# Retention and a mixture of experts on one core: q's factors computed on the chip, one tile's keys transposed instead of loaded, and a new order of work where the two stages meet

## The chip, the cores and the metric

The kernel runs on one core of one Trainium2 chip. The metric is the device time of one execution in microseconds (us), given as the median over several runs; the profile shows one execution.

The engines are TensorE (PE: matmuls; PEld are its loads of stationary operands, which overlap them), VectorE (DVE), ScalarE (ACT), GpSimd (POOL) and SyncE (SP, which here only issues transfers). Each works through its own instructions in order and waits on semaphores for the others.

## The reference

```python
def _attn_ref(q, k, v):                      # 8 batches, 8 heads, 576 positions, 64 per head
    scores = (1 / np.sqrt(D_)) * np.matmul(q, k.transpose(0, 1, 3, 2))
    gamma = 1.0 - 2.0 ** (-5.0 - np.arange(H))
    rel = pos[:, None] - pos[None, :]
    Dmat = np.where(rel >= 0, gamma[:, None, None] ** rel, 0.0)
    return np.matmul(scores * Dmat, v)       # retention: decay by distance, causal

def _moe_ref(x, w_gate, w_output_gate, w1, w2):   # x: 4608 tokens of 512; 8 experts, 1024 hidden
    logits = x @ w_gate
    e_idx = np.argmax(logits, axis=1)             # one expert per token
    gate_w = softmax(logits)[np.arange(N), e_idx]
    eom = sigmoid(x @ w_output_gate)
    for e in range(E):
        mask = e_idx == e
        ye = np.maximum(x[mask] @ w1[e], 0.0) @ w2[e]
        out[mask] = gate_w[mask, None] * eom[mask, e, None] * ye
```

## The kernel before

**Stage 1, retention.** The 4608 tokens are 36 tiles of 128 (`g` from 0 to 35); nine of them cover two sequences of 576 positions, so `c = g % 9` tells where a tile lies in its pair (`c = 4` holds the end of one and the start of the other, `c = 8` needs no update of the state). For each tile `load` brings `pk[g]`: q, k and v, q and k transposed. `scores` multiplies k by q into the PSUM tile `sc` (two banks), and VectorE masks it into `S_sb`. `by_state` adds what earlier tiles left in a running state, `outT` adds the tile's own part into `o_ps`, and VectorE multiplies `o_ps` by the decay factors of q, `gq_sb`, into `xT`. Those factors depend on the position in the sequence, so before the change five sets of 128 columns are loaded (one for each of `c` = 0 to 4; later tiles use columns shifted by 64). `update` adds the tile to the state with `kn[g]`, the keys by rows, and ScalarE copies the state out of PSUM (`stT`). `kn` comes in one of two ways: for odd `g` between 2 and 31 (`by_rows`) it is loaded by `load_k`, otherwise `k_rows` transposes it on TensorE into the one bank `k_ps` and ScalarE copies it. `prep` scales v on GpSimd (`vp`). `xnat` turns `xT` back into rows and forms the gating logits; ScalarE copies the rows into `xgrp`.

**Gating.** Every four tiles, `gate1a`, `gate1b`, `gate2`, `gate3a` and `gate3b` choose an expert and a slot for each token with small VectorE operations; `gate2` counts with matmuls into `k_ps`. The rows go by indirect scatters on GpSimd into `xs` in DRAM, which is ordered by expert. `gate4` works out which slots stay empty and adds scatters that fill them.

**Stage 2, experts.** An expert's rows are read back, transposed, and split into a high part `xh` (ScalarE) and a lower part `xl` (VectorE), and so are the weights; `mm1` makes three products for each block of weights (`xh`·`w1h`, `xl`·`w1h`, `xh`·`w1l`) and `mm2` likewise with `w2`. Each hidden block passes through ScalarE (`hh`) and VectorE (`hl`). The results are scattered to `out`.

**Where the stages meet.** Expert 0 starts before the last tiles are gated: its first 360 rows are three row tiles, transposed during the last three tiles of stage 1 by `transp(0, 0)`, `transp(0, 1)` and `transp(0, 2)`. `transp_hi` does the four transposes into a PSUM tile named by `pools["x_ps"]` and the high part, `transp_lo` the lower part. The first goes into `k_ps`, the second into the second bank of `sc`, the third into the first bank of `sc`. After them come `by_state(35)`, `outT(35)`, `xnat(34)` and the first `mm1(0, 0, 0)`, whose PSUM tiles lie where `sc`, `o_ps` and `k_ps` were.

**What sets the order.** In stage 1 and at the meeting (`tc.manual_schedule`), each engine executes instructions in the order in which the program writes them; only GpSimd's order is chosen by the scheduler at the meeting. All of SP's transfers go through one queue. Transfers take eight semaphores in turn, so that a transfer's issue waits until the eighth before it has landed. The start is written out in `load_first`; the rest of the constants follow in `load_rest(step)` at tiles 0 to 3.

Of the kernel before, what the change touches and what calls it, by code (L numbers as in the profile page):

```python
# [10 lines left out]
F32 = mybir.dt.float32  # L11
# [3 lines left out]
AF = mybir.ActivationFunctionType  # L15
ALU = mybir.AluOpType
# [17 lines left out]
TA = -(-CA // P)  # L34
SNAP = 5
# [13 lines left out]
def tile_retention_moe(  # L49
# [16 lines left out]
    V, A, G, T, SP = nc.vector, nc.scalar, nc.gpsimd, nc.tensor, nc.sync  # L66
# [16 lines left out]
    gk_sb = con_sb[:, 0:CPB * H].rearrange("p (c h a) -> p c h a", c=CPB, a=1)  # L83
    cmat_sb = con_sb[:, CPB * H:].rearrange("p (c a i) -> p c a i", c=4, a=1)
    ident = cmat_sb[:, 2, 0, :]
    gq_sb = const.tile([P, NP, 640], F32, name="gq_sb")
    iw = const.tile([P, NP, 144], F32, name="iw")
    cbf_sb = const.tile([P, 2, P], BF16, name="cbf_sb")
    csm_sb = const.tile([P, 16 + 2 * CT], F32, name="csm_sb")
    base2 = const.tile([P, 1, E], F32, name="base2")  # L90
    bump = const.tile([P, 1], F32, name="bump")
    tok_sb = const.tile([P, NTILE], I32, name="tok_sb")
# [8 lines left out]
    base = csm_sb[:, 8:16].rearrange("p (a e) -> p a e", a=1)  # L101

    stT = [const.tile([P, NP, D], F32, name=f"stT{i}") for i in range(2)]

    def load_rest(step):
        if step < 3:
            n = slice(P * (step + 2), P * (step + 3))
            SP.dma_start(out=gq_sb[:, :, n], in_=gq[:, :, n])
        if step == 0:
            for p in range(NP):  # L110
                o = 0 if p % 2 == 0 else 16
                A.copy(out=iw[:, p, o:o + P], in_=ident)
# [12 lines left out]
    const.tile([P, 16], F32, name="shift0")  # L125
    W1, W2 = {}, {}

    def start_w(which, e, fp):
# [92 lines left out]
    def transp(e, t):  # L221
        transp_lo(*transp_hi(e, t))
# [88 lines left out]
    def load_first():  # L311
        t = [ld.tile([P, 3, 512], F32, name="pk") for _ in range(4)]
        pk.update(enumerate(t))
        n = CPB * H + 2 * P
        SP.dma_start(out=t[0][:, 1], in_=pack[0, :, 1])
        A.dma_start(out=t[0][:, 0], in_=pack[0, :, 0])
        SP.dma_start(out=con_sb[:, 0:n], in_=cmat[:, 0:n])
        A.dma_start(out=t[0][:, 2], in_=pack[0, :, 2])
        SP.dma_start(out=con_sb[:, n:n + P], in_=cmat[:, n:n + P])
        A.dma_start(out=t[1][:, 0:2], in_=pack[1, :, 0:2])  # L320
        SP.dma_start(out=gq_sb[:, :, 0:P], in_=gq[:, :, 0:P])
        SP.dma_start(out=t[1][:, 2], in_=pack[1, :, 2])
        for i in (2, 3):
            if i == 3:
                SP.dma_start(out=gq_sb[:, :, P:2 * P], in_=gq[:, :, P:2 * P])
            SP.dma_start(out=t[i][:, 0:2], in_=pack[i, :, 0:2])
            SP.dma_start(out=t[i][:, 2], in_=pack[i, :, 2])
            if i == 2:
                wgv = wg.rearrange("(p c) g -> c p g", c=P)
                SP.dma_start(out=iw[:, 0:NP:2, P:144], in_=wgv[:, 0:NP:2])  # L330
                SP.dma_start(out=iw[:, 1:NP:2, 0:16], in_=wgv[:, 1:NP:2])

    def by_rows(g):
        return g % 2 == 1 and 1 < g < GT * SNAP + 12
# [77 lines left out]
    def outT(g, S_sb, state):  # L412
        o = o_ps
        c = g % CPB
        part = lambda p, r: o[64 * ((p + r) % 2):64 * ((p + r) % 2) + 64, r, P * (p // 2):P * (p // 2) + P]

        for r, p in ((r, p) for r in range(2) for p in range(NP)):
            T.matmul(part(p, r), lhsT=vs[g][:, 2 * p + r, :], rhs=S_sb[:, r, p, :],
                     start=(state is None and p < 2), stop=True, skip_group_check=True)
        x = wk.tile([P, NP, P], F32, name="xT")  # L420
        c0 = P * c if c < 5 else 64 + P * (c - 5)
        V.tensor_tensor(out=x.rearrange("p (r s) i -> p r s i", r=2),
                        in0=o[:, :, 0:2 * P].rearrange("p r (s i) -> p r s i", s=2),
                        in1=gq_sb[:, :, c0:c0 + P].rearrange("p (r s) i -> p r s i", r=2), op=ALU.mult)
        xT[g] = x

    def gate1a(n):
# [62 lines left out]
    def gate3b():  # L490
        n, oh, ex, zs = gt.pop("pend")
        sli = gt.pop("sl")
        x = xgrp[n % 2]
# [6 lines left out]
        V.reciprocal(out=x[:, :, DM + 1:DM + 2], in_=zs)  # L500
# [68 lines left out]
    pools["x_ps"] = lambda: ps_s.tile([P, NP, P], F32, name="k_ps").rearrange("p (b k) i -> p b k i", b=2)  # L569
    def scatters(n, pause):  # L570
        for f in todo[0:n]:

# [4 lines left out]
    with tc.manual_schedule():  # L577
        S_next = scores(0)
        k_rows(0)
        for g in range(NTILE):  # L580
# [15 lines left out]
            if g + 1 < NTILE:  # L596
                prep(g + 1)
                S_next = scores(g + 1)
            else:
                pools["x_ps"] = lambda: sc[:, 0].rearrange("p (b k i) -> p b k i", b=2, k=2)  # L600
                transp(0, 2)
            if g < NTILE - 1:

# [20 lines left out]
            weights_lo(g - 1, (1,))  # L624
            if g > 0:
                xnat(g - 1)
            if "sl" in gt:
                gate3b()
            if "fill" in gt and g == NTILE - 2:
                gate4()  # L630
            if g % GT == 0 and g > 0:
                gate1a(g // GT - 1)
            if g == NTILE - 1:
                wide = wk.tile([P, H, D], F32, name="vp")
            if g == NTILE - 1:
                scatters(len(todo), wide)
            if g in (NTILE - 3, NTILE - 2):
                if g == NTILE - 2:
                    pools["x_ps"] = lambda: sc[:, 1].rearrange("p (b k i) -> p b k i", b=2, k=2)
                transp(0, g - NTILE + 3)  # L640
    gt["after"] = list(scat)
    psctx.close()
    ps_h = mctx.enter_context(tc.tile_pool(name="ps_h", bufs=4, space=PSUM, side="right", reuse_waits="tile"))
# [196 lines left out]

def _consts():
    gam = 1.0 - 2.0 ** (-5.0 - np.arange(H, dtype=np.float64))
    s = np.concatenate([np.arange(S), np.arange(64)])
    gqh = gam[:, None] ** s[None, :] / np.sqrt(D)
    gq = np.repeat(gqh[np.array(SLOT)][:, :, None], D, axis=2).reshape(NP, P, 640).transpose(1, 0, 2)
    pos = (np.arange(CPB)[None, :] * P + np.arange(P)[:, None]) % S
# [52 lines left out]
```

## Time and profile before

| | |
|---|---|
| median of 3 runs | 612.72 us (611.83 to 613.25) |
| profiled execution, its own time | 608.3 us |
| span of that execution | 606.5 us |
| mean granted TensorE clock | 0.991 |
| busy: PE, PEld | 591.2 us (97%), 529.4 us (87%) |
| busy: DVE, ACT, POOL | 332.0 us (55%), 221.3 us (36%), 188.0 us (31%) |
| moved by transfers | 100.28 MB, mean 165 GB/s |
| stage 1 / stage 2 meet at | about 153 to 162 us from the span's start |

In the rows of the profile a line stands as L235; a line of the timeline gives start, duration, engine, line, operation, output <- inputs, how many instructions were merged, and in brackets the idle time before it and what ended it ("issue" is time in which nothing that the profile shows was waited for). The view of waits gives total, number and longest. The table by windows gives, for each stretch, the busy time of each engine, then the granted clock, the share of the 16 transfer engines that was busy (it can pass 1, since packets overlap) and GB/s. "PEld" rows are used for TensorE below where possible, since starts of loads are measured and ends of matmuls are modelled.

### The profile page before, as it was taken

Reading aid. Unit: us, or ns where it says so; the run is one execution under the profiler, and the core shown is the slowest. Engines: PE = TensorE matmul, PEld = TensorE weight load, DVE = VectorE, ACT = ScalarE, POOL = GpSimd, SP = SyncE. Lnnn points to the kernel's source line nnn. Section 1 sums busy time; section 2 is a strip of 40 time slices with the busy share of each in tenths; the row PEclk is TensorE's granted clock in tenths of the full one; section 3 lists DMA queues with packets and bytes.
Section 4 is the critical chain, followed back from the end, with each engine's and each line's share of the span. In section 5 each row is a group of like instructions: output and inputs, shape, how many; then the busy total and the mean of one; then the engine's idle time right before and its main releaser. Section 6 shows DMA issues by size and latency. Waiting matters only on the chain. (4 is left out here: it accounts for less than half of the span.)

```text
span 606.5 us, 13987 instructions
## 1 busy us (share of the span) xinstructions
PE 591.2 (97%) x5688; PEld 529.4 (87%) x5688; DVE 332.0 (55%) x731; ACT 221.3 (36%) x481; POOL 188.0 (31%) x235
## 2 busy tenths in 40 slices
PE   8899999999899999999999999999999999999995
PEld 6789889889798999879978987997899799889974
DVE  3498989898460666625543554445265435625410
ACT  3233444333231544325333443443354344325110
POOL 2245555575636524016013301601250110110011
PEclk9999999999799999999999999999999999999998
DMA  9988999995215676434343634444262335321011
GB/s 312 356 306 329 322 308 328 346 308 165 90 57 192 177 198 194 140 118 135 110 138 116 175 104 136 116 139 139 96 189 91 121 102 146 100 83 52 1 38 42
DMA packets 56925, 100.28 MB, mean 165 GB/s; under 512 B 14839, under 2 KB 35832, under 8 KB 56860
## 3 DMA queue, kind: packets, MB, share of 16 engines
q1 hardware_dynamic: 46988, 76.72, 39.9%
q0 software_dynamic: 9440, 21.60, 9.8%
q8 instruction: 45, 0.74, 0.5%
q10 hardware_dynamic: 432, 1.05, 0.5%
q14 instruction: 20, 0.16, 0.1%
HBM read 77.75 MB, written 31.18 MB: 180 GB/s over the span
## 5 line engine op out<-in xcount | busy, mean ns | idle before, releaser
L262 PE MATMUL h_ps<-xh,w1h 128*128 128x360 f32 (+1 forms) x512 | 155.4, 303 | 0.0
L262 PE MATMUL h_ps<-xh,w1l 128*128 128x360 f32 (+1 forms) x512 | 155.0, 303 | 0.0
L262 PE MATMUL h_ps<-xl,w1h 128*128 128x360 f32 (+1 forms) x512 | 154.9, 303 | 0.0
L289 POOL DMA_INDIRECT out_dram<-y,idx x40 | 39.7, 993 | 314.5 <-ACT y L288 269.5
L270 DVE SCALAR_TENSOR_TENSOR hl<-h_ps,hh 128x360 fp32r<-128x360 f32 (+1 forms) x128 | 61.3, 479 | 129.0 <-ACT hh L269 123.2
L283 PE MATMUL y_ps<-w2h,hh 128*128 128x512 f32 (+1 forms) x320 | 125.1, 391 | 0.0
L283 PE MATMUL y_ps<-w2l,hh 128*128 128x512 f32 (+1 forms) x320 | 125.0, 391 | 0.0
L283 PE MATMUL y_ps<-w2h,hl 128*128 128x512 f32 (+1 forms) x320 | 124.7, 390 | 0.0
L269 ACT ACTIVATE hh<-h_ps 128x360 fp32r<-128x360 f32 (+1 forms) x128 | 54.7, 427 | 118.0 <-PE h_ps L262 117.1
L262 PEld LDWEIGHTS h_ps<-xl,w1h 128*128 128x128 f32 x512 | 96.3, 188 | 0.3
L262 PEld LDWEIGHTS h_ps<-xh,w1h 128*128 128x128 f32 x512 | 96.3, 188 | 0.3
L262 PEld LDWEIGHTS h_ps<-xh,w1l 128*128 128x128 f32 x512 | 96.2, 188 | 0.0
L288 ACT ACTIVATE y<-y_ps,idx 128x512 f32<-128x512 f32 (+1 forms) x40 | 27.5, 688 | 138.8 <-issue 90.1
L147 DVE TENSOR_TENSOR w1l<-st,w1h 128x512 fp32r<-128x512 f32 x64 | 47.3, 776 | 48.2 <-ACT w1h L142 46.8
L283 PEld LDWEIGHTS y_ps<-w2h,hl 128*128 128x128 f32 (+1 forms) x320 | 58.8, 184 | 14.1
L283 PEld LDWEIGHTS y_ps<-w2h,hh 128*128 128x128 f32 (+1 forms) x320 | 58.9, 184 | 13.8
L283 PEld LDWEIGHTS y_ps<-w2l,hh 128*128 128x128 f32 (+1 forms) x320 | 58.8, 184 | 13.6
L354 POOL TENSOR_TENSOR vp<-pk,con_sb 128x512 f32<-128x512 f32 x36 | 37.4, 1040 | 54.5 <-PE st_ps L394 34.9
L194 POOL DMA_INDIRECT xs<-xgrp,sli x36 | 39.0, 1082 | 33.0 <-issue 17.1
L194 POOL DMA_INDIRECT xs<-zx,fill x42 | 45.2, 1077 | 7.1 <-issue 6.6
L147 DVE TENSOR_TENSOR w2l<-st,w2h 128x512 fp32r<-128x512 f32 x64 | 44.7, 736 | 2.3
L378 DVE TENSOR_TENSOR S_sb<-sc,con_sb 128x512 f32<-128x512 f32 x64 | 41.1, 683 | 7.1 <-PE sc L367 6.6
(128 smaller groups left out, 672.4 us busy)
## 6 DMA issues: line engine op xcount, KB each, us to landing
st<-in_w_dram SPq DMA_DIRECT2D x64, 512.0 KB
pk<-in_pack_dram SPq DMA_DIRECT2D x32, 768.0 KB
x_q<-xs SPq DMA_DIRECT2D x140, 64.0 KB
kn<-in_krow_dram SPq DMA_DIRECT2D x14, 256.0 KB
gq_sb<-in_gq_dram SPq DMA_DIRECT2D x5, 256.0 KB
pk<-in_pack_dram SPq DMA_DIRECT2D x4, 256.0 KB
pk<-in_pack_dram SPq DMA_DIRECT2D x2, 512.0 KB
x_g<-xs SPq DMA_DIRECT2D x4, 256.0 KB
```

The costliest lines, as they stand in the source:

```text
L147: V.tensor_tensor(out=lo[:, k], in0=st[:, k], in1=hi[:, k].bitcast(F32), op=ALU.subtract)
L194: i = G.indirect_dma_start(out=xs, out_offset=bass.IndirectOffsetOnAxis(ap=at, axis=0), in_=x, in_offset=None, **({} if bound is None else ...
L262: i = T.matmul(ps, lhsT=a[:, k, :], rhs=b[:, k, 0:n], start=(j == 0), stop=(j == 3 * KB - 1))
L269: A.activation(out=hh, in_=ps, func=AF.Relu)
L270: V.scalar_tensor_tensor(out=hl, in0=ps, scalar=0.0, in1=hh.bitcast(F32), op0=ALU.max, op1=ALU.subtract)
L283: i = T.matmul(ps, lhsT=a[:, n], rhs=b, start=(j == 0), stop=(j == 3 * FB - 1))
L288: A.activation(out=y, in_=ps, func=AF.Copy, scale=idx.bitcast(F32)[0:m, e, t, 1:2])
L289: G.indirect_dma_start(out=out, out_offset=bass.IndirectOffsetOnAxis(ap=idx[0:m, e, t, 0:1], axis=0), in_=y, in_offset=None, bounds_check= ...
L354: G.tensor_tensor(out=vs[g], in0=pk[g][:, 2].rearrange("p (h d) -> p h d", h=H), in1=gk_sb[:, g % CPB].broadcast_to([P, H, D]), op=ALU.mult)
L378: V.tensor_tensor(out=v(S_sb[:, r].rearrange("p a i -> p (a i)")), in0=v(sc[:, r]), in1=cmat_sb[:, 0:2].rearrange("p c a i -> p a (c i)"). ...
```

## The change

**q's factors.** `gq` is now one set of 128 by 512 plus a 16-column table `gam`. ScalarE makes sets 1 to 4 from set 0 at steps 0 to 3 of `load_rest`, each with four activations of 128 columns that multiply by one column of `gam` (step 3: eight of 64 columns, half of them by `back`, four columns that come with `csm_sb`). The positions of k's factors are shifted so that five sets serve all tiles (`c % 5`). Four loads of 256 KB go; the first becomes 128 rows of 2 KB, and `gam` (8 KB) is loaded ahead of tile 2.

**Tile 3's keys.** `by_rows` starts at 5, so tile 3's `kn` is transposed on TensorE and copied by ScalarE, and its load of 256 KB goes.

**The meeting.** The third row tile goes into `k_ps`. `gate3b` loses its tail (`gate3c`: the running counts `cum`), which for group 7 comes in tile 35's iteration together with `gate4`, so that VectorE does the lower parts first.

```diff
     def load_rest(step):
-        if step < 3:
-            n = slice(P * (step + 2), P * (step + 3))
-            SP.dma_start(out=gq_sb[:, :, n], in_=gq[:, :, n])
+        for k in range(NP):
+            n = P if step < 3 else 64
+            A.activation(out=gq_sb[:, step + 1, P * k:P * k + n], in_=gq_sb[:, 0, P * k:P * k + n], func=AF.Copy,
+                         scale=gam[:, NP * step + k:NP * step + k + 1])
+            if step == 3:
+                A.activation(out=gq_sb[:, 4, P * k + 64:P * k + P], in_=gq_sb[:, 0, P * k + 64:P * k + P],
+                             func=AF.Copy, scale=back[:, k:k + 1])
...
-        SP.dma_start(out=gq_sb[:, :, 0:P], in_=gq[:, :, 0:P])
+        SP.dma_start(out=gq_sb[:, 0], in_=gq[:, 0:DM])
         SP.dma_start(out=t[1][:, 2], in_=pack[1, :, 2])
         for i in (2, 3):
-            if i == 3:
-                SP.dma_start(out=gq_sb[:, :, P:2 * P], in_=gq[:, :, P:2 * P])
+            if i == 2:
+                SP.dma_start(out=gam, in_=gq[:, DM:DM + 16])
...
     def by_rows(g):
-        return g % 2 == 1 and 1 < g < GT * SNAP + 12
+        return g % 2 == 1 and 3 < g < GT * SNAP + 12
...
-                        in1=gq_sb[:, :, c0:c0 + P].rearrange("p (r s) i -> p r s i", r=2), op=ALU.mult)
+                        in1=gq_sb[:, c % 5].rearrange("p (r s i) -> p r s i", r=2, s=2), op=ALU.mult)
...
         todo.extend(partial(scatter_x, x[:, t, :], sli[:, t, :]) for t in range(GT))
+        gt["cum"] = (n, oh)
+        if n != NTILE // GT - 2:
+            gate3c()
+
+    def gate3c():
+        n, oh = gt.pop("cum")
...
             else:
-                pools["x_ps"] = lambda: sc[:, 0].rearrange("p (b k i) -> p b k i", b=2, k=2)
+                pools["x_ps"] = k_bank
                 transp(0, 2)
...
-            if "sl" in gt:
+            if "sl" in gt and g != NTILE - 2:
                 gate3b()
-            if "fill" in gt and g == NTILE - 2:
-                gate4()
...
             if g == NTILE - 1:
                 wide = wk.tile([P, H, D], F32, name="vp")
-            if g == NTILE - 1:
+                gate3c()
+                gate4()
                 scatters(len(todo), wide)
             if g in (NTILE - 3, NTILE - 2):
                 if g == NTILE - 2:
                     pools["x_ps"] = lambda: sc[:, 1].rearrange("p (b k i) -> p b k i", b=2, k=2)
-                transp(0, g - NTILE + 3)
+                x = transp_hi(0, g - NTILE + 3)
+                if "sl" in gt:
+                    gate3b()
+                transp_lo(*x)
```

TensorE (PE) where the stages meet, before: `x_g` are expert 0's rows, L235 the transposes of row tiles 1 and 2, L262 the first products of `mm1`.

```order
L531 MATMUL xb<-iw,xT 128x144 x2
L235 MATMUL sc<-con_sb,x_g 128x128 x4
L235 MATMUL sc<-con_sb,x_g 128x104 x4
L409 MATMUL o_ps<-pk,stT_93 64x128 x8
L418 MATMUL o_ps<-S_sb,vp 64x128 x8
L531 MATMUL xa<-iw,xT 128x144 x2
```

And after, at the same place (line numbers move: L235 is now L241, L409 is L415, L418 is L424, L531 is L542):

```order
L542 MATMUL xb<-iw,xT 128x144 x2
L241 MATMUL sc<-con_sb,x_g 128x128 x4
L241 MATMUL k_ps<-con_sb,x_g 128x104 x4
L415 MATMUL o_ps<-pk,stT_93 64x128 x8
L424 MATMUL o_ps<-S_sb,vp 64x128 x8
L542 MATMUL xa<-iw,xT 128x144 x2
```

The order on TensorE is the same; only the bank into which the last four transposes write has changed.

VectorE (DVE) at the same place, before: from `gate3b`'s last operation for the scattered rows, the reciprocal, through `gate3c`'s and `gate4`'s work (`ohs` to `fill`), to the lower parts `xl` of row tiles 1 and 2.

```order
L500 RECIPROCAL xgrp_91<-zs 128x4
L506 TENSOR_REDUCE ohs<-oh 128x8
L507 TENSOR_TENSOR cum<-cum,ohs 128x8
L515 TENSOR_TENSOR cnt<-cnt,bump 128x1
L207 TENSOR_TENSOR fl<-cnt,csm_sb 128x3
L212 TENSOR_TENSOR fo<-fl,csm_sb 128x3
L213 TENSOR_SCALAR fo<-fo 128x3
L217 TENSOR_TENSOR fl<-fl,fo 128x3
L218 TENSOR_TENSOR fill_2860<-fl,csm_sb 128x3
L245 TENSOR_TENSOR xl_2757<-sc,xh_2756 128x4x128
L245 TENSOR_TENSOR xl_2757<-sc,xh_2756 128x4x104
L422 TENSOR_TENSOR xT<-o_ps,gq_sb 128x512
```

And after, from the same reciprocal on:

```order
L505 RECIPROCAL xgrp_91<-zs 128x4
L251 TENSOR_TENSOR xl_2779<-sc,xh_2778 128x4x128
L251 TENSOR_TENSOR xl_2779<-k_ps,xh_2778 128x4x104
L427 TENSOR_TENSOR xT<-o_ps,gq_sb 128x512
L551 COPY lg<-xa 128x16
L552 TENSOR_TENSOR lg<-xb,lg 128x16
L517 TENSOR_REDUCE ohs<-oh 128x8
L518 TENSOR_TENSOR cum<-cum,ohs 128x8
L526 TENSOR_TENSOR cnt<-cnt,bump 128x1
```

Eight operations have moved from ahead of the two lower parts to behind `xT` and the logits of tile 34.

ScalarE (ACT) at the start, before: `k_ps` to `kn` is the copy of transposed keys, `iw` the identity that `xnat` uses, `stT` the state.

```order
L350 COPY kn<-k_ps 128x512
L112 COPY iw<-con_sb 128x128 x4
L396 COPY stT_93<-st_ps 128x256
L350 COPY kn<-k_ps 128x512
L396 COPY stT_94<-st_ps 128x256
```

And after:

```order
L356 COPY kn<-k_ps 128x512
L111 ACTIVATE gq_sb<-gq_sb,gam 128x128 x4
L119 COPY iw<-con_sb 128x128 x4
L402 COPY stT_93<-st_ps 128x256
L356 COPY kn<-k_ps 128x512
L111 ACTIVATE gq_sb<-gq_sb,gam 128x128 x4
L402 COPY stT_94<-st_ps 128x256
```

The activations stand ahead of the copies of the state in ScalarE's order; the first four need the loads of set 0 and of `gam`.

More of the change, by code (lines that the diff above doesn't have):

```diff
@@ L85, in tile_retention_moe @@
     ident = cmat_sb[:, 2, 0, :]
-    gq_sb = const.tile([P, NP, 640], F32, name="gq_sb")
+    gq_sb = const.tile([P, 5, DM], F32, name="gq_sb")
     iw = const.tile([P, NP, 144], F32, name="iw")
     cbf_sb = const.tile([P, 2, P], BF16, name="cbf_sb")
-    csm_sb = const.tile([P, 16 + 2 * CT], F32, name="csm_sb")
+    csm_sb = const.tile([P, 20 + 2 * CT], F32, name="csm_sb")
     base2 = const.tile([P, 1, E], F32, name="base2")
@@ L103, in tile_retention_moe @@
     stT = [const.tile([P, NP, D], F32, name=f"stT{i}") for i in range(2)]
+    gam = const.tile([P, 16], F32, name="gam")
+    back = csm_sb[:, 16 + 2 * CT:]
     def load_rest(step):
-        if step < 3:
-            n = slice(P * (step + 2), P * (step + 3))
-            SP.dma_start(out=gq_sb[:, :, n], in_=gq[:, :, n])
+        for k in range(NP):
[5 more added lines that the diff above has]
+                             func=AF.Copy, scale=back[:, k:k + 1])
         if step == 0:
@@ L121, in load_rest @@
             G.memset(zx.bitcast(I32)[:, DM:DM + 1], NT)
-    const.tile([P, 16], F32, name="shift0")
     W1, W2 = {}, {}
@@ L420, in outT @@
         x = wk.tile([P, NP, P], F32, name="xT")
-        c0 = P * c if c < 5 else 64 + P * (c - 5)
         V.tensor_tensor(out=x.rearrange("p (r s) i -> p r s i", r=2),
                         in0=o[:, :, 0:2 * P].rearrange("p r (s i) -> p r s i", s=2),
-                        in1=gq_sb[:, :, c0:c0 + P].rearrange("p (r s) i -> p r s i", r=2), op=ALU.mult)
+                        in1=gq_sb[:, c % 5].rearrange("p (r s i) -> p r s i", r=2, s=2), op=ALU.mult)
         xT[g] = x
@@ L567, in tile_retention_moe, with k_bank @@
     every = {mybir.EngineType.PE, mybir.EngineType.Activation, mybir.EngineType.DVE, mybir.EngineType.SP}
-    pools["x_ps"] = lambda: ps_s.tile([P, NP, P], F32, name="k_ps").rearrange("p (b k) i -> p b k i", b=2)
+    def k_bank():
+        return ps_s.tile([P, NP, P], F32, name="k_ps").rearrange("p (b k) i -> p b k i", b=2)
+    pools["x_ps"] = k_bank
     def scatters(n, pause):
@@ L599, in tile_retention_moe @@
             else:
-                pools["x_ps"] = lambda: sc[:, 0].rearrange("p (b k i) -> p b k i", b=2, k=2)
+                pools["x_ps"] = k_bank
                 transp(0, 2)
@@ L842, in _consts @@
     gam = 1.0 - 2.0 ** (-5.0 - np.arange(H, dtype=np.float64))
[L843 to L846, printed above, removed]
+    slots = lambda a: np.repeat(a[np.array(SLOT)][:, :, None], D, axis=2).reshape(NP, P, -1).transpose(1, 2, 0)
+    gq = slots(gam[:, None] ** np.arange(P)[None, :] / np.sqrt(D)).transpose(0, 2, 1).reshape(P, DM)
+    gt = slots(gam[:, None] ** (P * np.arange(1, 5))[None, :]).reshape(P, 4 * NP)
+    back = slots(gam[:, None] ** float(-P)).reshape(P, NP)
+    pos = np.arange(CPB)[None, :] * P + np.arange(P)[:, None]
+    pos = np.where(pos < S, pos, pos - S - 64)
     gk = gam[None, None, :] ** (-pos[:, :, None].astype(np.float64))
@@ L852, in _consts @@
     cbf = np.stack([(j < i), np.ones((P, P))], axis=1)
-    csm = np.zeros((P, 16 + 2 * CT))
+    csm = np.zeros((P, 20 + 2 * CT))
+    csm[:, 16 + 2 * CT:] = back
     csm[:, 16:16 + CT] = P * np.arange(CT)[None, :] + np.arange(P)[:, None]
-    csm[:, 16 + CT:] = [NT] + [CAP] * (CT - 1)
+    csm[:, 16 + CT:16 + 2 * CT] = [NT] + [CAP] * (CT - 1)
     csm[:, 0:8] = np.arange(8, 0, -1)
@@ L860, in _consts @@
     return {
-        "gq": np.ascontiguousarray(gq.astype(f)),
+        "gq": np.concatenate([gq, gt], axis=1).astype(f),
         "cmat": np.concatenate([gk.reshape(P, CPB * H), cmat.reshape(P, 4 * P)], axis=1).astype(f),
```

## The prediction

> **What bounds the kernel now.** I read the waits of TensorE first, because it is busy 97% of the span (table above): only time in which it stands still or runs slowly can be won. Its largest wait that is not at the start, by the starts of weight loads (total, number, longest), and the others that the change can touch:
>
> ```profile
> PEld o_ps L418 <- issue: 5.7, 27, 1.2
> PEld sc L235 <- DVE xl L245: 3.2, 1, 3.2
> PEld st_ps L394 <- DMA kn<-in_krow_dram: 1.2, 1, 1.2
> ```
>
> There is one wait of 3.2 us, for VectorE, where the transposes of expert 0's third row tile are due, and one of 1.2 us for the keys of a tile. Next the table by windows around the first one (busy us and count of PE, PEld, DVE, ACT, POOL, then the granted clock):
>
> ```profile
> 154.00:156.00 2.00, 0.00 (x0) 0.00 (x0) 1.79 (x12) 0.00 (x0) 0.95 (x1) 0.91 0.00 0
> ...
> 160.00:162.00 2.00, 2.00 (x11) 1.84 (x8) 0.76 (x2) 0.37 (x1) 1.77 (x3) 0.50 0.51 201
> 162.00:164.00 2.00, 2.00 (x12) 2.00 (x12) 0.28 (x2) 0.37 (x1) 1.84 (x3) 0.89 0.47 184
> ```
>
> The gap costs twice: the granted clock begins to fall inside it (0.91), and TensorE then works at 0.50 until shortly after 162 us. So I read the timeline of the weight loads there, a clean tile first and then the gap:
>
> ```profile
> 149.24 0.47 PEld L409 LDWEIGHTS o_ps<-pk,stT 64*64 64x64 f32 x16
> 149.88 0.85 PEld L418 LDWEIGHTS o_ps<-S_sb,vp 128*64 128x64 f32 x16 [0.17 <-issue]
> 150.70 0.60 PEld L394 LDWEIGHTS st_ps<-vp,kn 128*64 128x64 f32 x16
> ...
> 151.61 0.54 PEld L531 LDWEIGHTS xa<-iw,xT 128*128 128x128 f32 x4
> 152.09 0.56 PEld L531 LDWEIGHTS xb<-iw,xT 128*128 128x128 f32 x4
> 152.58 0.56 PEld L235 LDWEIGHTS sc<-con_sb,x_g 128*128 128x128 f32 x4
> 156.30 0.65 PEld L235 LDWEIGHTS sc<-con_sb,x_g 104*128 104x128 f32 x4 [3.15 <-DVE xl L245]
> 157.20 0.73 PEld L409 LDWEIGHTS o_ps<-pk,stT 64*64 64x64 f32 x16 [0.25 <-issue]
> 158.26 1.57 PEld L418 LDWEIGHTS o_ps<-S_sb,vp 128*64 128x64 f32 x16 [0.33 <-POOL vp L573]
> 160.16 0.98 PEld L531 LDWEIGHTS xa<-iw,xT 128*128 128x128 f32 x4 [0.33 <-issue]
> 161.05 1.06 PEld L531 LDWEIGHTS xb<-iw,xT 128*128 128x128 f32 x4
> 162.01 0.34 PEld L262 LDWEIGHTS h_ps<-xh,w1h 128*128 128x128 f32 x1
> ```
>
> The same instructions take about twice as long after the gap (L418 1.57 against 0.85 us). The gap itself ends with VectorE's first lower part, which stands behind the tail of gating:
>
> ```profile
> 152.48 0.15 DVE L480 COPY cnt<-k_ps 128x1 f32<-128x1 f32 x1
> ...
> 154.10 0.18 DVE L500 RECIPROCAL xgrp<-zs 128x4 f32<-128x4 f32 x1
> 154.19 0.18 DVE L506 TENSOR_REDUCE ohs<-oh 128x8 f32<-128x32 bf16 x1
> ...
> 155.48 0.16 DVE L218 TENSOR_TENSOR fill<-fl,csm_sb 128x3 int32<-128x3 f32 x1
> 155.56 0.68 DVE L245 TENSOR_TENSOR xl<-sc,xh 128x512 fp32r<-128x512 f32 x1
> 157.84 0.59 DVE L245 TENSOR_TENSOR xl<-sc,xh 128x416 fp32r<-128x416 f32 x1 [1.60 <-ACT xh L241]
> ```
>
> Both banks of `sc` are one tile, so the transposes into the first bank waited until VectorE had read the second.
>
> **The meeting of the stages (term A).** Before, TensorE needs from 152.58 to 162.01 = 9.43 us from the second row tile's transposes to the first product of expert 0. After, the third row tile goes to `k_ps`, whose last reader before it is the copy of the count, done at 152.48 + 0.15 = 152.63; the transposes are due at 152.58 + 0.56 = 153.14, so 0.5 us of margin. At full clock the same work is: two sets of transposes at 0.6 (0.56 and a little) = 1.2; L409 to L418 0.64 (149.24 to 149.88); L418 to the next group 0.82 (149.88 to 150.70); `xa` 0.48 (151.61 to 152.09); `xb` 0.49 (to 152.58): 3.63, say 3.65 us. That is a gain of 5.8 us, of which 3.15 is the gap and the rest the slow clock; the first products lose a little more in the half clock, so I take A = -5.9. Its cover: the first products at about 156.2 need both lower parts. VectorE, after the reciprocal at 154.28, needs 0.68 + 0.59 and is done at 155.55, 0.7 us early. The eight moved operations are 155.64 - 154.19 = 1.45 us; behind tile 34's logits they end near 158.6, ahead of the first `hl` at about 159 and of the fill scatter, GpSimd's fifth of the chain, that needs them. Ends for A: -3.15, if only the gap goes and the clock falls all the same; -6.2, if the smaller transposes (104 columns) are cheaper than I put them.
>
> [...]
>
> **Tile 3 (terms B and C).** Weight loads at tile 3, and the largest pause without a cause in the view of waits between 60 and 150 us:
>
> ```profile
> 21.68 0.20 PEld L418 LDWEIGHTS o_ps<-S_sb,vp 128*64 128x64 f32 x4 [1.21 <-issue]
> 23.05 0.55 PEld L394 LDWEIGHTS st_ps<-vp,kn 128*64 128x64 f32 x16 [1.17 <-DMA kn<-in_krow_dram]
> 23.66 0.42 PEld L348 LDWEIGHTS k_ps<-con_sb,pk 128*128 128x128 f32 x4
> ...
> PEld sc L367 <- issue: 0.7, 1, 0.7
> ```
>
> B: the load of tile 3's keys goes, and with it 1.17 us of waiting; four transposes come, 0.42 us on TensorE. ScalarE's extra copy falls into a stretch where it waits for TensorE. B = -0.75. C: the pause of 1.21 us at 21.68 has no cause in the profile. It stands where the transfer engines are fullest, and five transfers of 256 KB, 1.3 MB, go from ahead of it; but pauses of up to 0.7 us come later too, under a smaller load. Ends: 0 (it stays) and -1.2. By the nearest row, 0.7, I let it shrink to about half: C = -0.6.
>
> **ScalarE makes the factors (term D).** The rows at the start, and two durations for the price of a column as the factor:
>
> ```profile
> 7.28 0.90 ACT L112 COPY iw<-con_sb 128x128 f32<-128x128 f32 x4
> 8.68 1.04 POOL L354 TENSOR_TENSOR vp<-pk,con_sb 128x512 f32<-128x512 f32 x1 [2.00 <-DMA pk<-in_pack_dram]
> 9.75 0.37 ACT L396 COPY stT<-st_ps 128x256 f32<-128x256 f32 x1 [1.58 <-PE st_ps L394]
> 11.14 0.47 PEld L409 LDWEIGHTS o_ps<-pk,stT 64*64 64x64 f32 x16
> 13.39 0.37 ACT L396 COPY stT<-st_ps 128x256 f32<-128x256 f32 x1 [2.47 <-PE st_ps L394]
> ...
> L350 ACT COPY kn<-k_ps 128x512 f32<-128x512 f32 x18 | 10.5, 585 | 9.1 <-PE k_ps L348 6.2 <-DMA kn<-in_krow_dram 2.5
> L288 ACT ACTIVATE y<-y_ps,idx 128x512 f32<-128x512 f32 x2 | 1.4, 688 | 9.8 <-PE y_ps L283 9.8
> ```
>
> A factor per row costs 688 - 585 = 0.10 us more. The four copies of 128 columns take 0.90, so four such activations take about 1.3. [...] From 8.5: factors to 9.8, `iw` to 10.7, `stT` 0.37 to 11.07, needed at 11.14. There is no margin left, so each 0.1 us by which `gam` is later costs 0.1: behind it in ScalarE's order stand `stT` and the next `kn`, and TensorE waits for `stT`. D lies between 0 and +1.0; I take +0.2. At step 1 ScalarE stands idle 2.47 us before its copy of the state, more than the 1.3 us, and step 2 is alike; step 3 (eight of 64 columns, about 2 us) starts after tile 1's rows are copied, and tile 3's update, no longer stopped, ends about as late as they do: 0. The loads that go (four of 256 KB, and the keys) leave SP's queue earlier for the tiles behind; no wait of TensorE for them is left to gain.
>
> **What comes later (term E).** GpSimd's chain of seven scatters starts from the reciprocal and does not move, while TensorE is 5.9 us earlier. The last group's slots must wait until these scatters have landed, and TensorE's count (L717) waits for VectorE behind that.
>
> ```profile
> 165.14 0.98 POOL L194 DMA_INDIRECT xs<-zx,fill  x1 [0.16 <-issue]
> 174.50 0.17 DVE L485 CAST sli<-slf 128x4 int32<-128x4 f32 x1 [0.21 <-DVE slf L483]
> ...
> 180.39 0.96 POOL L194 DMA_INDIRECT xs<-xgrp,sli  x1 [0.30 <-issue]
> 183.27 0.93 SPq L162 DMA_DIRECT2D x_g<-xs  x2
> ```
>
> A scatter has landed by 183.27 - 181.35 = 1.92 us after GpSimd is done with it (what SP's load waits for), so the seventh by 166.12 + 1.92 = 168.04. The slots are due at 174.50 - 5.9 = 168.6. Margin 0.5 us; E = 0, at worst +0.5.
>
> **Sum.** A -5.9, B -0.75, C -0.6, D +0.2, E 0: -7.05 us. The profiled execution took 608.3 us, so it would take 601.3. The median of the runs is 612.72, 4.4 us above the profiled one; I keep the difference in microseconds: 605.7 us. A change within 0.2% (1.2 us) could not be told from none.
>
> **Rivals.**
> - The clock falls all the same. [...] Against it: at tile 3 two pauses of 1.2 us follow each other within 2.6 us, and the work behind them (0.42 us for four loads) is at full speed. A shrinks to -3.15, with the rest -4.3: 608.4 us.
> - A new wait at the meeting takes part of the gap's place: the count's copy or `xl` comes later than I count, say 0.5 to 2 us, without half a clock. For it: margins of 0.5 and 0.7 us. Against it: VectorE has no wait in this stretch that could lengthen it. About 607 us.
> - The change does not do what it says: the transposes still wait for the lower part, since the banks are bound together in another way. Against it: the writer of `k_ps` has only the count's copy ahead. Only B, C and D are left, -1.15: 611.6 us, no change that could be told.
> - Slower: E, as one mechanism. If the scatters landed not at 168.04 but 6 us later, TensorE would stand still at L717 for some 5.5 us, and the clock would halve behind it as it did at 156 us for another 2.8: +8.3 against -7.05, 614.0 us. It decides from about 4.7 us of delay on. Against it: the landing of 1.92 us is a measured row, and nothing adds to GpSimd's chain.
>
> **How the numbers follow.** Forecast 0.70, clock 0.10, new wait 0.11, change without effect 0.05, slower 0.04. The likeliest case reaches from A -6.2, C -1.2 and D 0 (-8.2: 604.5) to A -5.4, C 0, D +1.0, E +0.5 (-4.7: 608.0); a repeat of the median, by the spread of the runs, moves it 0.7 us either way. With the clock's case inside, and a little below for runs that the slow stretch cost more than the profiled one: 603.2 to 609.2. Faster by over 0.2%: forecast, clock and new wait, 0.91. Same 0.05, slower 0.04.
>
> **What would show it.** A: no wait at L241 over 0.3 us, the granted clock 1.00 in every window from 152 to 164 us, L424 at 0.85 us, and under 4 us from the second row tile's transposes to the first product. B: no wait of TensorE for `kn` before tile 5. C: no pause of over 0.7 us near 20 us. D: `by_state` of tile 1 starts no later than 11.4 us. E: under 0.6 us of waiting at the count (now L734). I am wrong if the clock still reads 0.50 there, or if TensorE waits over 1 us at the first product or at the count.

## The result, and the profile after

The changed kernel takes 606.53 us as a median of 6 runs (605.97 to 608.10), against 611.85 us of the kernel before on the same chip (611.22 to 613.25): ratio 0.9902, 95% interval 0.9881 to 0.9924. The forecast was 605.7 us, range 603.2 to 609.2. The profiled execution of after took 606.21 us (span 604.4, mean granted clock 0.997). The table ahead of the prediction has 608.3 us for the profiled execution of before; the medians differ by 5.3 us (the ratio makes it 6.0), the two profiles by only 2.1.

The waits of TensorE, after (total, number, longest):

```profile
PEld o_ps L424 <- issue: 4.6, 26, 0.3
PEld o_ps L415 <- issue: 3.0, 8, 0.6
...
PEld L734 <- DVE cum L518: 0.8, 1, 0.8
```

The 3.15 us for the lower part and the 1.17 us for tile 3's keys are gone. New is the second row: 3.0 us in pauses without a cause at `by_state` (L415), where before showed 0.2. The third is the count of the last group, 0.5 before.

The windows at the meeting, after (busy us of PE, PEld, DVE, ACT, POOL, then the granted clock):

```profile
154.00:156.00 2.00, 2.00 (x40) 1.93 (x37) 1.98 (x6) 0.74 (x2) 0.53 (x1) 1.00 0.00 0
156.00:158.00 2.00, 2.00 (x35) 1.73 (x35) 1.78 (x11) 1.37 (x3) 0.00 (x0) 1.00 0.03 8
158.00:160.00 2.00, 2.00 (x23) 1.83 (x20) 1.41 (x4) 0.56 (x2) 1.59 (x3) 1.00 0.12 49
```

The clock stays at 1.00. The timeline of the weight loads there, after:

```profile
155.75 0.56 PEld L241 LDWEIGHTS sc<-con_sb,x_g 128*128 128x128 f32 x4
156.23 0.57 PEld L241 LDWEIGHTS k_ps<-con_sb,x_g 104*128 104x128 f32 x4
156.90 0.43 PEld L415 LDWEIGHTS o_ps<-pk,stT 64*64 64x64 f32 x16
157.50 0.85 PEld L424 LDWEIGHTS o_ps<-S_sb,vp 128*64 128x64 f32 x16 [0.17 <-issue]
158.52 0.54 PEld L542 LDWEIGHTS xa<-iw,xT 128*128 128x128 f32 x4 [0.17 <-issue]
159.00 0.56 PEld L542 LDWEIGHTS xb<-iw,xT 128*128 128x128 f32 x4
159.49 0.19 PEld L268 LDWEIGHTS h_ps<-xh,w1h 128*128 128x128 f32 x1
```

From the second row tile's transposes to the first product it is 159.49 - 155.75 = 3.74 us; before 9.43. Tile 3 in the same view, after:

```profile
20.79 0.85 PEld L424 LDWEIGHTS o_ps<-S_sb,vp 128*64 128x64 f32 x16 [0.17 <-issue]
21.61 0.60 PEld L400 LDWEIGHTS st_ps<-vp,kn 128*64 128x64 f32 x16
22.28 0.42 PEld L354 LDWEIGHTS k_ps<-con_sb,pk 128*128 128x128 f32 x4
```

Neither the pause of 1.21 us nor the wait for the keys is left. Yet the second row tile's transposes come at 155.75, where they came at 152.58 before: stage 1 up to there is 3.2 us longer in this profile than in that one. This, and the share of each edit, is what the experiments are for.

### The profile page after: what moved, and what is told of

Its sections match the earlier page's. It is cut to its first block, busy times and chain, and to the rows that moved or that the text cites. A ratio compares the mean times of both kernels' runs of the same rounds, so it can differ in the third digit from the quotient of the medians.

```text
span 604.4 us, 14010 instructions
## 1 busy us (share of the span) xinstructions
PE 593.0 (98%) x5692; PEld 530.2 (88%) x5692; DVE 330.5 (55%) x731; ACT 226.0 (37%) x502; POOL 189.1 (31%) x235
## 5 line engine op out<-in xcount | busy, mean ns | idle before, releaser
L153 DVE TENSOR_TENSOR w1l<-st,w1h 128x512 fp32r<-128x512 f32 x64 | 44.5, 732 | 48.0 <-ACT w1h L148 44.2
L360 POOL TENSOR_TENSOR vp<-pk,con_sb 128x512 f32<-128x512 f32 x36 | 38.7, 1075 | 56.7 <-PE st_ps L400 35.1
```

Of the source, the lines that this page charges most:

```text
L153: V.tensor_tensor(out=lo[:, k], in0=st[:, k], in1=hi[:, k].bitcast(F32), op=ALU.subtract)
L360: G.tensor_tensor(out=vs[g], in0=pk[g][:, 2].rearrange("p (h d) -> p h d", h=H), in1=gk_sb[:, g % CPB].broadcast_to([P, H, D]), op=ALU.mult)
```

## The experiments

They were run as three sets, each on a chip of its own: runs 1 to 4 (before there: 610.93 us, 23 runs), 5 to 8 (607.26 us, 23 runs) and 9 to 12 (606.82 us, 11 runs). All ratios are against before on the same chip; a gain in us is worked out from the ratio, unless it is said to be between medians.

**1. The kernel before, once more** (no edit).

> The kernel before, unchanged, profiled once more. In the two profiles the stretch from the scores of tile 6 to those of tile 34 takes 114.7 us before the change and 118.9 after it, although its instructions are the same, while the medians of the runs lie 5.3 us apart and the profiled executions only 2.1. Theory 'chance': pauses of TensorE differ from execution to execution, and the profile of before was a lucky one; then this profile's stretch is 117 to 120 us, its time is 611 to 613, and the gap at the meeting is there again (9.4 us from the second row tile's transposes to the first product). Theory 'place': the pauses stand where blocks of instructions begin and belong to the kernel; then the stretch is 114.7 again within 0.5 us and the time is about 608 in this profile. Ratio to before 1.000.

Median 611.82 us, ratio 1.0003 (0.9992 to 1.0015). Its waits (profile of 612.27 us):

```profile
PEld o_ps L418 <- issue: 5.4, 25, 1.2
PEld sc L235 <- DVE xl L245: 3.2, 1, 3.2
PEld o_ps L409 <- issue: 3.1, 9, 0.5
...
PEld st_ps L394 <- DMA kn<-in_krow_dram: 0.4, 1, 0.4
```

The row for `by_state` in before's first profile was:

```profile
PEld o_ps L409 <- issue: 0.2, 1, 0.2
```

In run 1 the same kernel has pauses there too (3.1 us), and its wait for the keys is 0.4 us, not 1.17. From the scores of tile 6 to those of tile 34 it needs 118.6 us, as forecast by 'chance'. So the first profile had drawn a short stage 1 and a long wait for the keys; neither is a property of the code.

Windows at the meeting, same execution:

```profile
158.00:160.00 2.00, 0.00 (x0) 0.00 (x0) 1.79 (x10) 0.00 (x0) 1.13 (x2) 0.97 0.00 0
160.00:162.00 2.00, 1.88 (x20) 1.38 (x20) 0.40 (x2) 0.51 (x1) 1.83 (x3) 0.50 0.35 135
162.00:164.00 2.00, 2.00 (x21) 1.59 (x17) 0.25 (x1) 0.00 (x0) 1.67 (x4) 0.50 0.51 190
164.00:166.00 2.00, 2.00 (x11) 2.00 (x9) 0.87 (x2) 0.37 (x1) 1.83 (x3) 0.50 0.51 201
166.00:168.00 2.00, 2.00 (x12) 2.00 (x11) 0.18 (x1) 0.37 (x1) 1.84 (x3) 0.82 0.38 150
```

How long the half clock held can be worked out from these: 0.97 means that the last 0.12 us of that window ran at half (0.03 of 2 us, doubled), 0.82 the first 0.72 us, so from 159.88 to 166.72: 6.8 us. The first profile's windows give the same, 155.64 to 162.44. Over the 35 executions of before on this chip the mean granted clock falls into groups: 0.991 to 0.992 (7 of them, mean time 612.2 us), 0.993 to 0.994 (22, 611.3 us), 0.998 to 0.999 (6, 610.4 us). So the cost of the half clock is drawn anew each time: nothing in six of 35, 0.9 us in the middle group, and 612.2 - 610.4 = 1.8 us in the group of both profiles; weighted over the 35 it is 0.9 us. Putting the difference between the groups down to the clock alone is an estimate.

**2. The meeting alone.** Before, with the bank and the order (`gate3c` is split off as in the change; not shown again):

```diff
-                pools["x_ps"] = lambda: sc[:, 0].rearrange("p (b k i) -> p b k i", b=2, k=2)
+                pools["x_ps"] = k_bank
...
-            if "sl" in gt:
+            if "sl" in gt and g != NTILE - 2:
                 gate3b()
-            if "fill" in gt and g == NTILE - 2:
-                gate4()
...
-            if g == NTILE - 1:
+                gate3c()
+                gate4()
...
-                transp(0, g - NTILE + 3)
+                x = transp_hi(0, g - NTILE + 3)
+                if "sl" in gt:
+                    gate3b()
+                transp_lo(*x)
```

> Before with only the edits at the meeting: the third row tile into the keys' bank, the lower parts ahead of gating's counts. My sum says -5.9 us (ratio 0.990), 3.8 us instead of 9.4 from the second row tile's transposes to the first product, and the clock at 1.00 throughout. Rival: the gain of the whole change came from the start and the meeting is worth only the gap, -3.2 us (0.995).

606.80 us, ratio 0.9930 (0.9914 to 0.9947): -4.3 us. In the profile the meeting, from the second row tile's transposes to the first product, is 159.74 - 156.00 = 3.74 us, as in after:

```profile
156.00 0.56 PEld L235 LDWEIGHTS sc<-con_sb,x_g 128*128 128x128 f32 x4
...
159.74 0.19 PEld L262 LDWEIGHTS h_ps<-xh,w1h 128*128 128x128 f32 x1
```

All runs lie at 0.997 or more in the mean clock. Their mean is 606.7 us; the six executions of before at 0.998 to 0.999 on this chip took 610.4. So the gap without a half clock costs 3.7 us, a little more than its 3.15.

**3. The start alone.** After, with the bank and the order of before.

> After without the edits at the meeting: q's factors on ScalarE and tile 3's keys transposed. My sum says -1.15 us (ratio 0.998). Theory 'place': eight more instructions of TensorE ahead of tile 4 move every later block, the stretch from tile 6 to tile 34 takes 118.9 us as in the profile of after, and the time is +3 us against before (1.005). Theory 'chance': no such loss, ratio 0.997 to 0.999.

610.77 us, ratio 0.9991 (0.9976 to 1.0006): -0.55 us, a gain that can't be told from none, against -1.15 of B, C and D. Pause and wait at tile 3 are gone; tile 2 starts 0.4 us later than in run 1. Runs 2 and 3 together give 4.8 us of the whole change's gain, for which the ratios have 6.0 (first result) and 4.9 (run 9).

**4. Tile 6's keys loaded.** After, with one more load by rows, so that the number of TensorE's instructions ahead of tile 7 is that of before.

```diff
-        return g % 2 == 1 and 3 < g < GT * SNAP + 12
+        return g == 6 or g % 2 == 1 and 3 < g < GT * SNAP + 12
```

> After, but tile 6's keys are loaded instead of transposed, so that from tile 7 on TensorE's instructions stand at the same count as in before; four transposes less. Theory 'place': the pauses at tiles 15, 19, 23 and 27 go, the stretch from tile 6 to tile 34 is about 114.5 us, and the time is 4 us below after's (ratio to before about 0.984). Theory 'chance': the time is after's within 1 us (ratio 0.989 to 0.991).

606.26 us, ratio 0.9917 (0.9899 to 0.9936); the pauses at `by_state` stay (2.5 us against 3.0), and the stretch from tile 6 to tile 34 is 119.5 us, where 'place' had forecast 114.5. That they come from where the instructions lie in the program is refuted. What they go with is the set of runs: in the next two sets, each on another chip, the same kernels have hardly any (one row of 0.5 us in run 5, quoted below), and before takes 4 us less.

**5. The bank alone.** Before, with only the third row tile's bank changed (the first line of the diff in run 2).

> The kernel before with one edit: the third row tile's transposes go into the bank of k_ps; VectorE's order stays (the tail of gating ahead of the lower parts). Theory: the wait of 3.15 us at the transposes (L239 here, L235 before) goes wholly, and the granted clock stays at 1.00 from 152 to 164 us in every execution. The lower parts come as late as before (first one begins near 155.6, second ends near 156.9 us), the first products are due near 156.2 to 156.5, so up to 0.6 us is waited for xl at the first products. Gain 3.6 to 4.3 us on the median: ratio 0.9930 to 0.9941, mean clock 0.996 or more in all runs. Rival (the two edits are needed together, the lower part stands in the way again): a wait for xl of 1.5 to 3 us comes at the first products, the clock falls there, and less than 2.5 us is gained, ratio over 0.996.

602.66 us, ratio 0.9931 (0.9917 to 0.9946): the whole gain of the meeting without the new order. Its waits:

```profile
PEld o_ps L409 <- issue: 0.5, 1, 0.5
...
PEld h_ps L262 <- DVE xl L245: 0.2, 1, 0.2
```

The late lower parts cost 0.25 us at the first products. The granted clock is 1.00 at the meeting. The profiled execution (604.71 us, the slowest of the five) had its half clock elsewhere, at tile 3. Timeline of the weight loads there:

```profile
20.25 0.63 PEld L418 LDWEIGHTS o_ps<-S_sb,vp 128*64 128x64 f32 x12 [0.17 <-issue]
22.09 0.20 PEld L418 LDWEIGHTS o_ps<-S_sb,vp 128*64 128x64 f32 x4 [1.21 <-issue]
23.22 0.85 PEld L394 LDWEIGHTS st_ps<-vp,kn 128*64 128x64 f32 x16 [0.93 <-DMA kn<-in_krow_dram]
24.19 0.72 PEld L348 LDWEIGHTS k_ps<-con_sb,pk 128*128 128x128 f32 x4
24.89 1.03 PEld L531 LDWEIGHTS xa<-iw,xT 128*128 128x128 f32 x4
```

And the windows there, same execution:

```profile
22.00:24.00 2.00, 1.22 (x20) 0.98 (x20) 0.69 (x1) 0.00 (x0) 0.00 (x0) 0.84 0.98 380
24.00:26.00 2.00, 2.00 (x14) 1.88 (x11) 0.00 (x0) 0.96 (x2) 1.04 (x1) 0.50 0.73 252
26.00:28.00 2.00, 2.00 (x54) 1.84 (x52) 0.37 (x3) 0.74 (x2) 0.00 (x0) 0.81 0.89 253
```

The pause and the wait, 1.21 and 0.93 us with four loads between them, were followed by the half clock, by the same working from 23.36 to 26.76 us: 3.4 us, half as long as in run 1. I had expected a mean clock of 0.996 or more in all runs; this one has 0.995. The prediction had taken such a pair as evidence that short pauses don't halve the clock, and in the profiles of before and of runs 1, 2, 6 and 7 the clock stays at 1.00 behind a like pair (1.1 to 1.4 and 0.3 to 1.2 us). So such a pair can do it; it did in one of six profiles.

**6. The order alone.** Before, with the lower parts ahead of the counts and the third row tile still in `sc` (without the first line of the diff in run 2).

> The kernel before with the other edit of the meeting: the lower parts ahead of the counts on VectorE; the third row tile still goes into the bank of sc and waits for the first lower part. [...] Gain 1.3 from the gap and about 1 us from the clock on the median: ratio 0.9955 to 0.997, mean clock 0.996 or more in all runs. [...]

605.00 us, ratio 0.9972 (0.9957 to 0.9986). Its wait at the transposes, from the view of waits:

```profile
PEld sc L235 <- DVE xl L245: 1.8, 1, 1.8
```

The windows behind it, same execution:

```profile
154.00:156.00 2.00, 1.44 (x20) 1.11 (x20) 0.64 (x2) 0.51 (x1) 1.30 (x2) 0.86 0.00 0
156.00:158.00 2.00, 2.00 (x20) 1.57 (x16) 0.45 (x1) 0.00 (x0) 1.71 (x3) 0.50 0.42 161
158.00:160.00 2.00, 2.00 (x14) 2.00 (x13) 0.87 (x2) 0.67 (x2) 1.79 (x3) 0.78 0.53 199
```

The gap shrank by about the 1.3 us expected, from 3.15 to 1.8 us, and the clock fell all the same in this execution, from 155.44 to 158.88 us: 3.4 us again. Of the 12 runs six have a mean clock of 0.993 to 0.994 (mean 606.2 us) and six 0.996 to 0.998 (604.1 us). I had expected 0.996 or more in all of them; about half lie below. The mean clock does not say where in the execution it fell. But of the 47 executions without the gap (after and runs 2, 4, 5, 9, 10, 11 and 12) only two lie under 0.996, so that nearly all of the six are the gap's.

**7. The gap made longer.** Before, with eight more reductions on VectorE ahead of the lower part:

```diff
+        if n == NTILE // GT - 2:
+            for _ in range(8):
+                V.tensor_reduce(out=ohs, in_=oh.rearrange("p t e -> p e t"), op=ALU.add, axis=AX.X)
```

> The kernel before with eight more VectorE reductions (each a repeat of the one that sums the experts' marks, 0.14 to 0.18 us) ahead of the lower part, so that the gap of 3.15 us becomes 4.3 to 4.6 us. [...] Rival (whether the clock falls is decided by something other than the gap's length): about one run in six still shows 0.997 or more, and the median rises by 1.2 to 1.45 us alone.

610.34 us, ratio 1.0054 (1.0038 to 1.0069): +3.3 us. Its wait at the transposes:

```profile
PEld sc L235 <- DVE xl L245: 5.6, 1, 5.6
```

The gap grew by 2.4 us, more than I had priced (the eight took 1.88 us together, and one operation behind them 0.67 instead of 0.18). All five runs have a mean clock of 0.991, where the rival had about one in six at 0.997 or more. Of the 3.3 us, 0.9 is more than the gap. The lower clock accounts for about as much: the two executions of before at 0.991 and 0.992 on this chip took 608.3 us, 1.0 above the median.

**8. Tile 3's keys alone.** Before, with `by_rows` from 5.

> The kernel before with one edit at the start: tile 3's keys are transposed instead of loaded; q's factors are loaded as before. Theory (the pause of 1.2 us without a cause in tile 3 belongs to TensorE's own instructions there, which the four transposes shift): the pause and the wait for the loaded keys (0.3 to 0.4 us in the later executions) both go, the transposes cost 0.42, net 1.1 to 1.2 us by the start of tile 5, ratio 0.998 to 0.9985; then q's factors cost 0.5 to 0.7 us in the change, which gained 0.55 us with both. Rival (the pause came from the five loads of 256 KB ahead of it, so that q's factors removed it): the pause stays at 1.2 us here and the ratio is 1.000 within 0.0012.

607.15 us, ratio 0.9995 (0.9980 to 1.0009): the rival's number. Timeline at tile 3:

```profile
21.11 0.42 PEld L418 LDWEIGHTS o_ps<-S_sb,vp 128*64 128x64 f32 x8 [0.17 <-issue]
22.82 0.42 PEld L418 LDWEIGHTS o_ps<-S_sb,vp 128*64 128x64 f32 x8 [1.29 <-issue]
23.20 0.60 PEld L394 LDWEIGHTS st_ps<-vp,kn 128*64 128x64 f32 x16
```

The wait for the keys went, the pause stayed. It now comes after 8 loads of `outT` instead of 12, and four transposes stand ahead of it that were not there: it stays at the same count of TensorE's instructions from the start, behind the 344th weight load in both profiles, counted from the first scores (5.18 us in both).

**9 to 12. The parts together, on one chip.** The changed kernel again; the same with tile 3's keys loaded (`1 < g` in `by_rows`); this with VectorE's order of before; and the changed kernel with q's factors loaded as before. The diff of run 10 against the changed kernel:

```diff
-        return g % 2 == 1 and 3 < g < GT * SNAP + 12
+        return g % 2 == 1 and 1 < g < GT * SNAP + 12
```

> The changed kernel once more, on the chip of the next three, so that they can be compared with it. Theory (what is won is the meeting's 3.6 us and half clock, and at tile 3 the pause of 1.2 us): ratio 0.990 to 0.9925 whichever of the two levels the time of the kernel before has on this chip; no pause of over 0.7 us before 25 us; mean clock 0.996 or more in all runs.

> The changed kernel with tile 3's keys loaded again: q's factors from ScalarE and the meeting's edits alone. Theory (the pause in tile 3 came from q's loads, so it goes here too; the keys, with three loads of 256 KB fewer ahead of them, land in time): no pause of over 0.7 us near 20 us, a wait for the keys of 0.4 us at most, no transposes (0.42 us): 0 to 0.7 us faster than the changed kernel. Rival (the keys land when they did, and TensorE, without the pause, waits for them about 1.2 us longer than before): a wait for the keys of 1.2 to 2 us, and 0.5 to 1.5 us slower than the changed kernel.

> As the run with q's factors and the meeting, but VectorE's order at the meeting as before: only the bank of the third row tile is changed there. Theory (the bank alone takes the wait away, as the run with it alone showed, and the order saves at most the 0.25 us for xl at the first products): within 0.4 us of the run with q's factors and both edits of the meeting, and the wait for the lower part under 0.4 us. Rival (with the start earlier the order matters): over 0.8 us slower than that run, with a wait for xl of over 0.6 us.

> The kernel before with the meeting's edits and tile 3's keys transposed; q's factors are loaded as before. Theory (q's loads make the pause): the pause of 1.2 to 1.3 us in tile 3 stands as in the run with the keys alone, and the time is 0.8 to 1.6 us above the changed kernel's, ratio 0.9925 to 0.9945. Rival (q's factors from ScalarE cost at the start about what they save): within 0.5 us of the changed kernel.

| run | q by ScalarE | tile 3's keys transposed | bank | order | median us | ratio |
|---|---|---|---|---|---|---|
| 9, after | yes | yes | yes | yes | 602.53 | 0.9920 (0.9891 to 0.9950) |
| 10 | yes | no | yes | yes | 601.23 | 0.9899 (0.9872 to 0.9926) |
| 11 | yes | no | yes | no | 601.40 | 0.9904 (0.9877 to 0.9932) |
| 12 | no | yes | yes | yes | 602.90 | 0.9929 (0.9901 to 0.9956) |

Run 10 beats both kernels, by the medians: 5.6 us below before, 1.3 below after. The intervals of runs 9 and 10 overlap, but only one of run 9's six times lies within the range of run 10's. Run 10's timeline at tile 3:

```profile
20.17 0.85 PEld L424 LDWEIGHTS o_ps<-S_sb,vp 128*64 128x64 f32 x16 [0.17 <-issue]
20.99 0.60 PEld L400 LDWEIGHTS st_ps<-vp,kn 128*64 128x64 f32 x16
21.66 0.42 PEld L354 LDWEIGHTS k_ps<-con_sb,pk 128*128 128x128 f32 x4
```

With q's loads out of the queue the loaded keys are there in time and there is no pause: q's edit, which takes four loads of 256 KB out, was enough for both, so the rival (a longer wait for the keys) is out. In run 12, which loads q's factors, the pause stands (timeline of the weight loads):

```profile
22.22 0.42 PEld L418 LDWEIGHTS o_ps<-S_sb,vp 128*64 128x64 f32 x8 [1.31 <-issue]
```

Run 11 is within 0.2 us of run 10: the order adds nothing that can be told where the bank is changed. Run 12 is only 0.4 us above run 9, which is the rival's number; the trace shows more, 24.84 against 24.08 us at tile 5's first load, of which run 9's pauses further on took some back.

Run 9 missed two of its marks. One of its six runs has a mean clock of 0.995 (604.64 us), where I had expected 0.996 or more in all; it was not the profiled one, so that the place of the fall is not known. And TensorE's wait at the count of the last group is longer than in after, because the slots ahead of it wait for a transfer (view of waits, then the timeline of VectorE):

```profile
PEld L734 <- DVE cum L518: 1.2, 1, 1.2
...
168.69 0.17 DVE L490 CAST sli<-slf 128x4 int32<-128x4 f32 x1 [0.94 <-DMA xs<-zx,fill]
```

What this means for term E stands below.

## Why the prediction was right, point by point

The median and the range held, and so did the direction and most of the mechanism. The gain did not come out as summed: 7.05 us were forecast, 5.3 measured between medians. A was 1.6 us too large; B gained nothing and C twice its term, so these two about made up for each other. That the time is only 0.8 us off is in part luck: the median of before itself came out 0.9 us lower with three more runs (611.85 against 612.72).

- **A, the meeting: right in mechanism, too large for a median.** Sized at -5.9 from one profile with the half clock; such executions did lose that (9.44 to 3.74 us in the profiles of runs 1 and 2, and 612.27 to 606.16 us in all). By the ratios the gain is 4.3 us (run 2) and 4.2 (run 5), near what run 1's set gives by its means, 3.7 for the gap and 0.9 for the half clock. The step that failed is "of which 3.15 is the gap and the rest the slow clock": the 2.75 us of slow clock was carried over to every run, while it is drawn anew in each, and the profile had drawn the long one of 6.8 us. Even that group lost 1.8 us by the times, not 2.75. The forecast of the meeting's length (3.65 us) met 3.74, and the margins of 0.5 and 0.7 us held. That the order is needed for it was assumed, not weighed: the bank alone gives the gain, at 0.25 us of waiting.
- **B, tile 3's keys: the step failed.** The wait of 1.17 us came from one execution (0.3 to 1.1 in runs 1, 2, 5, 6 and 7), and the removal of q's loads takes it away without this edit (run 10). What the edit itself leaves is the 0.42 us of transposes, against it: with q's factors made on the chip it makes the kernel slower, by 0.4 us in the trace and 1.3 us between the medians of runs 9 and 10. The rest of the 1.3 is not settled; in run 9's profile there are longer pauses without a cause at later tiles, and the 1.2 us at the count against 0.8 in run 10.
- **C, the pause: right edit, half the size.** Taken at half, -0.6; it went (to 0.2 us at most) in all six traces with q's factors from ScalarE and stood at 1.1 to 1.4 us in all eight with q's factors loaded. The transfers ahead of it, which the prediction named, are the likely cause: q's edit takes four of them away. That it is they, and not ScalarE's new work, no run shows apart; removing the fifth, the keys' load, left the pause (runs 8 and 12). Its fixed place in TensorE's instructions is shown by run 8; what the engine waits for there is not.
- **D, ScalarE's factors: right, within its range.** The activations waited for `gam`, as the row of ScalarE in after shows, and took the 1.3 us forecast:

```profile
8.71 1.28 ACT L111 ACTIVATE gq_sb<-gq_sb,gam 128x128 f32<-128x128 f32 x4 [0.53 <-DMA gam<-in_gq_dram]
```

  The start at 8.5 us, from which the prediction counted, is shown by no run: the four began at 8.71 us here, at 9.11 in run 3 and at 9.18 in run 4. `by_state` of tile 1 started at 11.70 us, not by 11.4: later by 0.56 than before's first profile, of which tile 0's own scores took most. Run 8, which loads q's factors, has 11.70 too. Over all profiles it starts at 11.1 to 11.7 us with the factors loaded (mean 11.5) and at 11.5 to 12.0 with them from ScalarE (mean 11.7), which is the +0.2 forecast. With B and C it made -0.55 us in run 3.
- **E, the count: mis-sized, and the margin did not hold each time.** Forecast were 0, at worst +0.5, and under 0.6 us of waiting. In after it waits 0.8 us. It is 0.8 also in run 3, without the meeting's edits, and in runs 4, 10 and 11, and 0.5 in every profile that loads q's factors, with the meeting's edits (runs 2 and 12) or without. So 0.3 us goes with q's edit and not with the earlier TensorE. In after's VectorE row for the slots the wait names VectorE itself, with no transfer in it:

```profile
172.09 0.17 DVE L490 CAST sli<-slf 128x4 int32<-128x4 f32 x1 [0.57 <-DVE slf L488]
```

  Why it waits 0.57 us there, and 0.21 before, stays open. In run 9, the same kernel, it is 0.94 us and the row names the scatters: GpSimd was done with the seventh at 165.55 us, and the slots came at 168.69, 3.1 us later, where the prediction had put the landing at 1.92. There TensorE waited 1.2 us at the count, more than the 1 us that the prediction had named as a sign of being wrong. So the mechanism of the rival 'slower' occurs, at 0.4 us over run 10's count and not at 5.5. E was 0.3 us in after's profile and 0.7 in run 9's.
- **The 4.4 us between profile and median** were kept in microseconds, and this held the forecast. The first profile had a stage 1 without the pauses; with after's 8 pauses at `by_state` (3.0 us) the profiled gain was 2.1 us, and the one between medians 5.3. Had I taken the profile's sum for the time, 601.3 us would have been 5 too low. The prediction gave no reason for keeping the difference; it was luck that it lay in tiles 6 to 34 (114.7 us in that profile, 118.6 in run 1), where the change does nothing.
- **The rival on the clock** did not come: the gap is gone. Had 1.8 us of the gap been left, its chance of 0.10 would have been too small: at that length the mean clock was 0.994 or less in 6 of 12 executions, and the profiled one fell to 0.50 (run 6).

The clock fell in more of the executions where the gap was longer. By the mean clock (0.995 or less) it fell, in the second set, in 6 of 12 executions at 1.8 us (run 6), 26 of 35 at 3.15 us (before and run 8) and 5 of 5 at 5.6 us (run 7); in the first set in 29 of 35 at 3.15 us. In the profiles of runs 5 and 6 it fell to 0.50 with no more than 1.2 + 0.9 and 1.8 us of standing still. The half clock lasted 3.4 us in runs 5, 6 and 8, and twice that in before and in runs 1, 3 and 7 (6.8 us). Why it falls in one execution and not in the next is not shown.

## What to carry to other kernels

In this kernel a stall of 1.8 to 3.15 us on TensorE cost its length and, in some runs, a half clock (by the mean clock 6 of 12 at 1.8 us, 29 of 35 at 3.15 us in the first set): price the length fully and the clock by how many of the timed runs show it in their mean clock, not by the one that was profiled. Before two edits are made for one stall, ask of each whether the other leaves it anything: here q's edit also freed the keys, and the bank alone did what bank and order were to do. A pause "without a cause" of 1.1 to 1.4 us that appeared at the same place in all eight profiles with q's factors loaded could be removed; those that came and went between sets of runs did not move with the edits made here. And a margin of 0.5 us on the landing of a transfer, read from one row, is not safe: a second profile of the same kernel had it 1.2 us later.

## What the runs showed of the hardware that was not expected

- The same program had two levels of stage 1. From the scores of tile 6 to those of tile 34 it took 118 to 119.5 us in the profiles of the first set and of after, and 114 to 115.2 in those of runs 5 to 12; the pauses at `by_state` sum to 2.5 to 3.1 us in the former, and to 0.5 us or less in all of runs 5 to 12; before took 610.93 us in the first set, and 607.26 and 606.82 us in the others. Before's first profile (114.7 us, 608.3 in all at a mean clock of 0.991) is of the lower level, although the timed runs beside it are of the upper; executions of before at 0.991 and 0.992 took 608.2 and 608.3 in the second set. The program does not decide it, as run 4 shows; that it is the chip is possible from three sets, not shown.
- The granted clock fell to 0.50 after 1.8 us without work (run 6), and once after two pauses of 1.2 and 0.9 us with four loads between them (run 5). It then stayed there for 3.4 or for 6.8 us, nothing between in the profiles, which fits the groups of the mean clock in run 1.
- A pause of 1.1 to 1.4 us at one place of TensorE's instructions stood in eight traces and was gone in the six with q's edit, although none of TensorE's instructions there waits on the loads that went. What the engine waits for is not shown.
- From the end of GpSimd's last scatter ahead of the slots to the slots it was 3.1 us in run 9; the prediction's row for a landing had 1.92.
